# Weight conversion with its scratch in PSUM, and pair sums over fixed buffers, in an attention and gated-convolution kernel

## The chip, the cores and the metric

The kernel runs on one core of a Trainium2 chip. Its time is device microseconds (us) of one launch. A core has five engines with a queue each: TensorE (PE; PEld is its loading of stationary operands), VectorE (DVE), ScalarE (ACT), GpSimd (POOL) and SyncE (SP), which issues DMA transfers. Each works through its queue in order and waits on semaphores for the others. SBUF is the working memory, PSUM the memory that TensorE writes its results to. GpSimd has no operand in PSUM anywhere in this kernel.

## What is computed

Attention over 4 batches, 8 heads, 768 positions and 64 values a head, in which a query sees only the keys with the same 6 sign bits of a projection; then a gated feed-forward with a causal convolution of five taps.

```python
q_bits = (np.einsum('bhsd,dk->bhsk', q, proj) > 0)      # k_bits alike
mask = q_bucket[:, :, :, None] == k_bucket[:, :, None, :]
scores = np.where(mask, scale * np.matmul(q, k.transpose(0, 1, 3, 2)), -1000000000.0)
attn = np.exp(scores - np.max(scores, axis=-1, keepdims=True))
attn = attn / (np.sum(attn, axis=-1, keepdims=True) + 1e-09)
x = np.matmul(attn, v)                                   # heads side by side: (4, 768, 512)
gate_pre = sum(conv_w[k] * xp[:, k:k + S, :] for k in range(5))
out = (1.0 / (1.0 + np.exp(-gate_pre)) * (x @ w_val)) @ w_out
```

`w_val`, `w_out` (512 x 512 each) and `conv_w` arrive as float64, so the kernel receives them as 64-bit words and has to make fp32 out of them.

## The kernel before

The work is cut into 192 tiles: 32 units (batch, head) times 6 blocks of 128 queries. One step k of the main loop issues, for tile k: the row maximum over 768 scores on VectorE (`maxima`, L253), a factor and a shift a row (`factors` L259, `shifts` L263), the scores of tile k+1 on TensorE (`scores`, L247, two buffers `s` in PSUM), the exponentials on ScalarE with their row sum (`exponentials`, L271); every second step, for the pair of tiles k-2 and k-1, the row sums plus 1e-9 (`row_sums`, L277) and their reciprocal (`recip`, L281); for tile k-2 the division on GpSimd (`normalise`, L286); for tile k-3 the transposes on TensorE (L295, two halves of three, in two PSUM buffers `tp`), copied out by ScalarE in the step after (`keep_transposed`, L304). The product with the values (`attn_v`, L318), the split of its result into a high and a low part (`pair_x`, L338 and L339), the convolution (L347 and L349), and the feed-forward of a finished batch (`moe`, L380 and L405) are generators, and each step of the loop runs a step or a few of each.

The order in every queue is thus the order in which the Python code runs. It is written out by hand for TensorE, ScalarE, VectorE and GpSimd; the order of SyncE's transfers is found by the scheduler.

The conversion of the weights consists of eight parts of 128 x 512 (four of `w_val`, four of `w_out`). For each part a transfer of 512 KB brings the 64-bit words to a tile `w` (two buffers); ScalarE takes the magnitude of the upper word read as a float (L90, to a tile `o` in SBUF); VectorE bounds it from below (L92), shifts its bits (L93), joins them with the sign and exponent (L96), masks (L99) and scales the lower word (L100), then copies the high part out (L108); GpSimd forms the low part in two steps (L110, L112). The small `conv_w` takes the first five of these with 20 elements a row and an addition (L126). Two streams of four parts each take turns, and the loop runs (1, 0, 2, 0, 2, 2)[k % 6] steps from k = 0 on.

The sign bits of four heads at a time (`bits`, L203 and L206, twice half a row) go through one PSUM tile: `m` while no batch is in the feed-forward, else one of the two `tp` buffers. The tile `m` (one buffer) is otherwise the accumulator of the feed-forward, which begins after the first batch.

Of the kernel before, what the change touches and what calls it, by code (L numbers as in the profile page):

```python
# [8 lines left out]
FP32 = mybir.dt.float32  # L9
FP32R = mybir.dt.float32r  # L10
AF = mybir.ActivationFunctionType
ALU = mybir.AluOpType
AX = mybir.AxisListType
PSUM = bass.MemoryType.PSUM

I32 = mybir.dt.int32
# [10 lines left out]
def kernel(  # L27
# [49 lines left out]
    first = const.tile([P, 1], FP32, name="first")  # L77
    nc.scalar.activation(out=first, in_=ident[:, 0:1], func=AF.Exp)
    cw_sb = const.tile([P, NP * KW], FP32, name="cw_sb")

    wv = [const.tile([P, NP, 512], FP32R, name=f"wv{i}") for i in range(2)]
    wo = [const.tile([P, NP, 512], FP32R, name=f"wo{i}") for i in range(2)]

    def from_float64(w, t):

        lo, hi = w[:, :, 0], w[:, :, 1]
        a, d, ti = hi.bitcast(FP32), lo.bitcast(FP32), t.bitcast(I32)
        nc.scalar.activation(out=t, in_=a, func=AF.Abs)  # L90
        yield
        nc.vector.tensor_scalar(out=t, in0=t, scalar1=LEAST, scalar2=None, op0=ALU.max)  # L92
        nc.vector.tensor_scalar(out=ti, in0=ti, scalar1=3, scalar2=0x3fffffff,  # L93
                                op0=ALU.logical_shift_left, op1=ALU.bitwise_and)
        yield
        nc.vector.scalar_tensor_tensor(out=hi, in0=hi, scalar=-2 ** 30, in1=ti,  # L96
                                       op0=ALU.bitwise_and, op1=ALU.bitwise_or)
        yield
        nc.vector.tensor_scalar(out=ti, in0=hi, scalar1=-2 ** 23, scalar2=None, op0=ALU.bitwise_and)  # L99
        nc.vector.scalar_tensor_tensor(out=d, in0=lo.bitcast(U32), scalar=2.0 ** -52, in1=t,  # L100
                                       op0=ALU.mult, op1=ALU.mult)
        return a, d

    def split_weight(w, hi, lo):
        if w.dtype == I32:
            a, d = yield from from_float64(w, op.tile([P, 512], FP32, name="o"))
            yield
            nc.vector.tensor_copy(out=hi, in_=a)  # L108
            yield
            nc.gpsimd.tensor_tensor(out=a, in0=a, in1=hi.bitcast(FP32), op=ALU.subtract)  # L110
            yield
            nc.gpsimd.tensor_tensor(out=lo, in0=a, in1=d, op=ALU.add)  # L112
        else:
            nc.scalar.copy(out=hi, in_=w)
            yield
            nc.gpsimd.tensor_tensor(out=lo, in0=w, in1=hi.bitcast(FP32), op=ALU.subtract)

    def load_conv():
        if conv_w.dtype == mybir.dt.int64:
            w = const.tile([P, NP * KW, 2], I32, name="cw64")  # L120
            nc.sync.dma_start(out=w, in_=conv_w.bitcast(I32).rearrange("p (n t) -> p n t", t=2))
            t = const.tile([P, NP * KW], FP32, name="cwt")
            yield
            a, d = yield from from_float64(w, t)
            yield
            nc.vector.tensor_tensor(out=cw_sb, in0=d, in1=a, op=ALU.add)  # L126
        else:
            nc.sync.dma_start(out=cw_sb, in_=conv_w)

    def load_weights(which):  # L130
        parts = [(src[:, c, :], hl[0][:, c, :], hl[1][:, c, :])
                 for src, hl in ((w_val, wv), (w_out, wo)) for c in range(NP)]
        for src, hi, lo in parts[which::2]:
            if src.dtype == mybir.dt.int64:
                w = wst.tile([P, 512, 2], I32, name="w64")
                nc.sync.dma_start(out=w, in_=src.bitcast(I32).rearrange("p (n t) -> p n t", t=2))
            else:
                w = wst.tile([P, 512], FP32, name="w32")
                nc.sync.dma_start(out=w, in_=src)
            yield  # L140
            yield from split_weight(w, hi, lo)

    def load_raw(i):
        if i < len(units):
# [43 lines left out]
            yield from bits(i + 1)  # L188

    def side_tile():  # L190
        if not moes:
            return ps_m.tile([P, 512], FP32, name="m")
        return ps_t.tile([P, 512], FP32, name="tp")

    def bits(i):
# [69 lines left out]
    def exponentials(k):  # L265
        s, nb = ss.pop(k), nbs.pop(k)
        p = pp.tile([P, 2, HS], FP32, name="p")
        if k % 2 == 0:
            cur["sm"] = small.tile([P, 2, 2], FP32, name="sm")
        sm = cur["sm"]  # L270
        nc.scalar.activation(out=p, in_=s[:, :, 0:HS], func=AF.Exp, bias=nb, scale=gs.pop(k), accum_out=sm[:, k % 2, 0:1])  # L271
        ps[k] = (p.rearrange("p a b -> p (a b)"), sm)


    def row_sums(k):
        sums[k] = small.tile([P, 2, 2], FP32, name="s1")
        nc.vector.tensor_scalar(out=sums[k][:, :, 0], in0=ps[k][1][:, :, 0], scalar1=1e-9, scalar2=None, op0=ALU.add)  # L277

    def recip(k):
        ri = small.tile([P, 2], FP32, name="ri")  # L280
        nc.vector.reciprocal(out=ri, in_=sums.pop(k)[:, :, 0])  # L281
        rcs[k], rcs[k + 1] = ri[:, 0:1], ri[:, 1:2]

    def normalise(k):
# [80 lines left out]
    def moe(b, xs_, g):  # L365
        hs = {}
        todo = []

        def later():
            while todo:  # L370
                todo.pop(0)()

        def val(o, j):
            acc = acc_tile()
            m = 0
            for wi, xi in ((0, 0), (1, 0), (0, 1)):
                if m:
                    yield
                for c in range(NP):
                    nc.tensor.matmul(out=acc[:, 0:HS], lhsT=wv[wi][:, c, j * P:(j + 1) * P],  # L380
                                     rhs=xs_[(c, o)][xi], start=(m == 0), stop=(m == 11))
                    m += 1
                later()
            ht = hp.tile([P, HS], FP32, name="ht", bufs=2)
            nc.vector.tensor_tensor(out=ht, in0=acc[:, 0:HS], in1=g[j][:, o:o + HS], op=ALU.mult)  # L385

            def split():
                hh = hp.tile([P, HS], FP32R, name="hh")
                nc.vector.tensor_copy(out=hh, in_=ht)  # L389
                hl = hp.tile([P, HS], FP32R, name="hl")  # L390
                nc.gpsimd.tensor_tensor(out=hl, in0=ht, in1=hh.bitcast(FP32), op=ALU.subtract)  # L391
                hs[(o, j)] = (hh, hl)
            todo.append(split)
            yield

        def outp(o, tb):
            for gens in weights:
                finish(gens)
            acc = acc_tile()
            m = 0  # L400
            for hi, wi in ((0, 0), (0, 1), (1, 0)):
                if m:
                    yield
                for j in range(NP):
                    nc.tensor.matmul(out=acc, lhsT=hs[(o, j)][hi][:, tb * P:(tb + 1) * P],  # L405
                                     rhs=wo[wi][:, j, :], start=(m == 0), stop=(m == 11))
                    m += 1
                later()
            ob = op.tile([P, 512], FP32, name="o")
            if cur["gates"]:  # L410
                nc.vector.tensor_copy(out=ob, in_=acc)
            else:
                nc.scalar.copy(out=ob, in_=acc)
            r0 = o + tb * P
            nc.sync.dma_start(out=out[b, r0:r0 + P, :], in_=ob)
            yield

        def idle(n):
            for _ in range(n):
                later()  # L420
                yield

        def hold():
            while len(moes) < 2 and not cur["end"]:
                yield

        chunks = [(val, 0, j) for j in range(NP)]
        chunks += [(val, HS, 0)] + [(outp, 0, tb) for tb in range(3)] + [(val, HS, j) for j in range(1, NP)]
        chunks += [(idle, 2)] + [(outp, HS, tb) for tb in range(3)]
        if b < B - 1:  # L430
            chunks.insert(-2, (hold,))
        for f, *args in chunks:
            yield from f(*args)
# [9 lines left out]
    def step(gens):  # L443

        while gens:
            try:
                return next(gens[0])
            except StopIteration:
                gens.pop(0)

    def finish(gens):
        while gens:
            step(gens)
# [3 lines left out]
    with tc.manual_schedule(engines=ENGINES):  # L457
# [1 line left out]
            load_raw(i)  # L459
        load_values(0)  # L460
        first_prep()
        weights = [[load_conv(), load_weights(0)], [load_weights(1)]]
        first_signs()
        preps = [prep(1)]
        step(preps)
        scores(0)
        load_raw(5)
        step(weights[0])
        step(weights[1])
        turn = 0  # L470
        for k in range(N + LAG + 1):
            if 0 <= k - LAG - 1:
                keep_transposed(k - LAG - 1)
# [19 lines left out]
                exponentials(k)  # L493
            if k >= 60 or k % 2:
                step(convs)
            for _ in range((1, 0, 2, 0, 2, 2)[k % 6]):
                step(weights[turn])
                turn = 1 - turn
            for _ in range(3 if cur["gates"] else 1):
                step(moes)  # L500
            cur["gates"] = max(0, cur["gates"] - 1)
# [73 lines left out]
```

## Time and profile before

| | us |
|---|---|
| median of 3 runs | 630.7 |
| lowest and highest of them | 625.79, 632.56 |
| the profiled execution | 629.21 |
| its span, first to last instruction | 627.4 |
| busy: TensorE, VectorE, ScalarE, GpSimd | 591.0, 448.6, 421.2, 388.2 |

All shares and durations below are of that one profiled execution. A row of a group gives the line, the engine, the operation, what it writes and reads, how often, its busy time, the mean of one in ns, and the idle time of the engine just before it with what ended it. A row of a wait gives who waited for whom, the total, how often, and the longest. In order of time a row is a start, a duration, and what ran. Profiled spans on GpSimd are rough, and the ends of matmuls are modelled.

### The profile page before, as it was taken

Reading aid. Unit: us, or ns where it says so; the run is one execution under the profiler, and the core shown is the slowest. Engines: PE = TensorE matmul, PEld = TensorE weight load, DVE = VectorE, ACT = ScalarE, POOL = GpSimd, SP = SyncE. Lnnn points to the kernel's source line nnn. Section 1 sums busy time; section 2 is a strip of 40 time slices with the busy share of each in tenths; the row PEclk is TensorE's granted clock in tenths of the full one; section 3 lists DMA queues with packets and bytes.
Section 4 is the critical chain, followed back from the end, with each engine's and each line's share of the span. In section 5 each row is a group of like instructions: output and inputs, shape, how many; then the busy total and the mean of one; then the engine's idle time right before and its main releaser. Section 6 shows DMA issues by size and latency. Waiting matters only on the chain.

```text
span 627.4 us, 10639 instructions
## 1 busy us (share of the span) xinstructions
PE 591.0 (94%) x3496; PEld 425.8 (68%) x3496; DVE 448.6 (72%) x1032; ACT 421.2 (67%) x881; POOL 388.2 (62%) x358
## 2 busy tenths in 40 slices
PE   5799889989999999999999999999999999999997
PEld 2766556556667877677667777676667777776895
DVE  5879897989876857577676867569674877665532
ACT  3777767677788767577787667667788667675400
POOL 4677878687966856476655767367663677544221
PEclk9799988989999999999999999999999999999999
DMA  8542625343433343233434233243422224200111
GB/s 269 129 133 60 175 64 140 91 137 82 116 75 100 81 102 82 75 89 101 114 83 119 53 82 103 72 120 82 122 56 69 56 51 92 75 18 2 50 51 50
DMA packets 23270, 56.77 MB, mean 90 GB/s; under 512 B 4296, under 2 KB 4296, under 8 KB 23216
## 3 DMA queue, kind: packets, MB, share of 16 engines
q1 hardware_dynamic: 23072, 56.06, 33.7%
q8 instruction: 28, 0.46, 0.3%
q14 instruction: 26, 0.21, 0.1%
q10 hardware_dynamic: 144, 0.03, 0.0%
HBM read 23.12 MB, written 6.29 MB: 47 GB/s over the span
## 4 chain that ended last, share of the span: by engine, by line
PE 68%; DVE 13%; ACT 12%; DMA 3%; issue 2%; POOL 1%; SPq 0%; ACTq 0%; POOLq 0%; DVEq 0%
PE av L318 18%; PE s L247 16%; PE tp L295 12%; PE m L405 8%; PE m L380 7%; ACT p L271 5%; DVE nm L253 4%; ACT pt L304 4%; ACT x L326 2%; PE tp L380 1%; PE tp L405 1%; PE s L405 1%; DVE g L349 1%; DVE o L93 1%; PE tp L203 1%
## 5 line engine op out<-in xcount | busy, mean ns | idle before, releaser
L286 POOL TENSOR_SCALAR p<-p,ri 128x768 f32<-128x768 f32 x192 | 216.6, 1132 | 165.8 <-DVE nb L263 141.6
L253 DVE TENSOR_REDUCE nm<-s 128x1 f32<-128x768 f32 x192 | 182.5, 951 | 63.5 <-PE s L247 63.3
L304 ACT COPY pt<-tp 128x384 f32<-128x384 f32 x384 | 166.3, 485 | 84.2 <-PE tp L295 83.3
L271 ACT ACTIVATE p<-s,nb,gs 128x768 f32<-128x768 f32 x192 | 192.7, 1003 | 43.2 <-DVE nb L263 40.2
L295 PEld LDWEIGHTS tp<-ident,p 128*128 128x128 f32 x1152 | 131.6, 143 | 73.0 <-issue 45.7
L295 PE MATMUL tp<-ident,p 128*128 128x128 f32 x1152 | 166.8, 281 | 3.4 <-DVE u L206 1.5
L318 PE MATMUL av<-pt,vt 128*64 128x384 f32 x768 | 147.6, 506 | 0.0
L247 PE MATMUL s<-ak,aq 76*128 76x384 f32 x384 | 118.1, 389 | 23.9 <-ACT p L271 23.2
L247 PE MATMUL s<-bk,bq 128*128 128x384 f32 x384 | 100.6, 343 | 0.0
L318 PEld LDWEIGHTS av<-pt,vt 128*64 128x64 f32 x768 | 47.6, 137 | 63.8 <-issue 62.9
L247 PEld LDWEIGHTS s<-ak,aq 76*128 76x128 f32 x384 | 59.2, 194 | 38.0 <-ACT p L271 36.8
L349 DVE SCALAR_TENSOR_TENSOR g<-x,cw_sb,g 128x768 f32<-128x768 f32 x64 | 78.0, 1218 | 0.2
L247 PEld LDWEIGHTS s<-bk,bq 128*128 128x128 f32 x384 | 71.6, 193 | 0.0
L391 POOL TENSOR_TENSOR hl<-ht,hh 128x384 fp32r<-128x384 f32 x32 | 32.2, 1007 | 45.8 <-DVE hh L389 45.8
L169 POOL TENSOR_TENSOR bq<-r,aq 128x768 fp32r<-128x768 f32 x31 | 58.0, 1871 | 0.1
L326 ACT COPY x<-av 64x384 f32<-64x384 f32 x64 | 30.4, 475 | 34.0 <-PE av L318 33.3
L380 PE MATMUL m<-xh,wv 128*128 128x384 f32 x200 | 42.7, 337 | 0.0
L263 DVE TENSOR_SCALAR nb<-nm,gs 128x1 f32<-128x1 f32 x192 | 39.9, 208 | 3.5
L339 POOL TENSOR_TENSOR xl<-x,xh 128x384 fp32r<-128x384 f32 x32 | 33.6, 1067 | 12.2 <-DVE xh L338 12.2
L385 DVE TENSOR_TENSOR ht<-m,g 128x384 f32<-128x384 f32 x25 | 13.9, 556 | 35.3 <-PE m L380 32.0
L271 ACT ACTIVATION_READ_ACCUMULATOR p<-s,nb,gs 128x1 f32 x192 | 39.1, 204 | 0.0
L405 PE MATMUL m<-wo,hh 128*128 128x512 f32 x144 | 38.1, 394 | 0.0
(90 smaller groups left out, 489.8 us busy)
## 6 DMA issues: line engine op xcount, KB each, us to landing
r<-in_qk_dram SPq DMA_DIRECT2D x32, 384.0 KB
vt<-in_v_dram SPq DMA_DIRECT2D x16, 384.0 KB
out_dram<-o SPq DMA_DIRECT2D x24, 256.0 KB
ak<-aq SPq DMA_DIRECT2D x31, 192.0 KB
bk<-aq SPq DMA_DIRECT2D x31, 192.0 KB
bk<-bq SPq DMA_DIRECT2D x31, 192.0 KB
bq<-aq SPq DMA_DIRECT2D x31, 192.0 KB
w<-in_w_val_dram SPq DMA_DIRECT2D x4, 512.0 KB
```

The costliest lines, as they stand in the source:

```text
L169: nc.gpsimd.tensor_tensor(out=bq, in0=r, in1=aq.bitcast(FP32), op=ALU.subtract)
L247: nc.tensor.matmul(out=s[:, hf, 0:HS], lhsT=lq[0:n, qs], rhs=rk[0:n, hf * HS:(hf + 1) * HS], start=n == M, stop=n == P)
L253: nc.vector.tensor_reduce(out=nm, in_=s[:, :, 0:HS], axis=AX.XY, op=ALU.max, negate=True)
L271: nc.scalar.activation(out=p, in_=s[:, :, 0:HS], func=AF.Exp, bias=nb, scale=gs.pop(k), accum_out=sm[:, k % 2, 0:1])
L286: nc.gpsimd.tensor_scalar(out=p, in0=p, scalar1=rcs.pop(k), scalar2=1.0, op0=ALU.mult, op1=ALU.mult)
L295: nc.tensor.transpose(out=tp[:, n * P:(n + 1) * P], in_=p[:, kb * P:(kb + 1) * P], identity=ident)
L304: nc.scalar.copy(out=pt[:, :, qo:qo + P], in_=tp[:, 0:HS].rearrange("p (a b) -> p a b", b=P))
L318: nc.tensor.matmul(out=av[s * D:(s + 1) * D, 0:HS], lhsT=vt[:, kb, hh * D:(hh + 1) * D], rhs=pt[kb // 3][:, kb % 3, :], start=(kb == 0), s ...
L326: nc.scalar.copy(out=x[hh * D:(hh + 1) * D, o:o + HS], in_=av[s * D:(s + 1) * D, 0:HS])
L349: nc.vector.scalar_tensor_tensor(out=g, in0=x[:, k:k + S], scalar=w, in1=g, op0=ALU.mult, op1=ALU.add)
L380: nc.tensor.matmul(out=acc[:, 0:HS], lhsT=wv[wi][:, c, j * P:(j + 1) * P], rhs=xs_[(c, o)][xi], start=(m == 0), stop=(m == 11))
L405: nc.tensor.matmul(out=acc, lhsT=hs[(o, j)][hi][:, tb * P:(tb + 1) * P], rhs=wo[wi][:, j, :], start=(m == 0), stop=(m == 11))
```

## The change

Three things change.

The conversion's scratch moves. The magnitude stays in the SBUF tile `o`, and what VectorE makes from it (L97, L98, L104, and read by L101 and L105) lies in the PSUM tile `m`. The magnitude of the next part is taken one part ahead (`ahead`), right after GpSimd's first step of the part before, and its transfer is asked for after L101 of the part before. There is one stream instead of two, and no step of it runs before k = 8. The steps a turn are the same from there on.

The sums of the signs always go through a `tp` buffer, since `m` is now the scratch.

The row sums of a pair of tiles go to one of four fixed tiles `sm` of 2 x 2 elements a row, filled with 1e-9 once. The exponentials write column 0, the constant stays in column 1, and the addition of 1e-9 becomes a sum along the last axis (L298).

```diff
+    sms = [const.tile([P, 2, 2], FP32, name=f"sm{i}") for i in range(4)]
+    for sm in sms:
+        nc.gpsimd.memset(sm, 1e-9)
...
+    def magnitudes(w, t):
+        nc.scalar.activation(out=t, in_=w[:, :, 1].bitcast(FP32), func=AF.Abs)
+        return t
...
-        nc.scalar.activation(out=t, in_=a, func=AF.Abs)
-        yield
-        nc.vector.tensor_scalar(out=t, in0=t, scalar1=LEAST, scalar2=None, op0=ALU.max)
+        nc.vector.tensor_scalar(out=t, in0=m, scalar1=LEAST, scalar2=None, op0=ALU.max)
...
-            a, d = yield from from_float64(w, op.tile([P, 512], FP32, name="o"))
+            a, d = yield from from_float64(w, m, ps_m.tile([P, 512], FP32, name="m"))
...
             nc.gpsimd.tensor_tensor(out=a, in0=a, in1=hi.bitcast(FP32), op=ALU.subtract)
+            ahead()
             yield
...
+        def ahead():
+            if loads:
+                w = loads.pop(0)
+                m = magnitudes(w, op.tile([P, 512], FP32, name="o")) if w.dtype == I32 else None
+                ready.append((w, m))
+
+        loads = [fetch(parts[0][0])]
+        yield
+        ahead()
+        for n, (_, hi, lo) in enumerate(parts):
+            yield
+            for i, _ in enumerate(split_weight(*ready.pop(0), hi, lo, ahead)):
+                if i == 1 and n + 1 < len(parts):
+                    loads.append(fetch(parts[n + 1][0]))
+                yield
...
     def side_tile():
-        if not moes:
-            return ps_m.tile([P, 512], FP32, name="m")
         return ps_t.tile([P, 512], FP32, name="tp")
...
-        if k % 2 == 0:
-            cur["sm"] = small.tile([P, 2, 2], FP32, name="sm")
-        sm = cur["sm"]
+        sm = sms[k // 2 % 4]
...
-        sums[k] = small.tile([P, 2, 2], FP32, name="s1")
-        nc.vector.tensor_scalar(out=sums[k][:, :, 0], in0=ps[k][1][:, :, 0], scalar1=1e-9, scalar2=None, op0=ALU.add)
+        sums[k] = small.tile([P, 2], FP32, name="s1")
+        nc.vector.tensor_reduce(out=sums[k], in_=ps[k][1], axis=AX.X, op=ALU.add)
...
-        weights = [[load_conv(), load_weights(0)], [load_weights(1)]]
+        weights = [load_conv(), load_weights()]
...
-            for _ in range((1, 0, 2, 0, 2, 2)[k % 6]):
-                step(weights[turn])
-                turn = 1 - turn
+            for _ in range((1, 0, 2, 0, 2, 2)[k % 6] if k >= 8 else 0):
+                step(weights)
```

VectorE's queue among the first tiles, from the maximum of tile 6 to that of tile 7, before (`nm` is the negated maximum, `gs` and `nb` factor and shift, `ri` the reciprocal; numbers behind a name tell buffers apart):

```order
L253 TENSOR_REDUCE nm<-s 128x1
L277 TENSOR_SCALAR s_339<-sm 128x2
L259 TENSOR_SCALAR gs<-nm 128x1
L281 RECIPROCAL ri<-s_339 128x2
L263 TENSOR_SCALAR nb<-nm,gs 128x1
L99 TENSOR_SCALAR o<-w_186 128x512
L100 SCALAR_TENSOR_TENSOR w_186<-w_186,o 128x512
```

and the same tile after:

```order
L276 TENSOR_REDUCE nm<-s 128x1
L298 TENSOR_REDUCE s_333<-sm_120 128x2
L282 TENSOR_SCALAR gs<-nm 128x1
L302 RECIPROCAL ri<-s_333 128x2
L286 TENSOR_SCALAR nb<-nm,gs 128x1
```

The two conversion steps between the shift of tile 6 and the maximum of tile 7 are gone from there; the addition of L277 is the sum of L298.

VectorE's queue at tile 38, behind the shift, where a part of `w_out` and the first half of the signs meet, before:

```order
L281 RECIPROCAL ri<-s_1474 128x2
L263 TENSOR_SCALAR nb<-nm,gs 128x1
L99 TENSOR_SCALAR o<-w_1273 128x512
L100 SCALAR_TENSOR_TENSOR w_1273<-w_1273,o 128x512
L206 TENSOR_SCALAR u<-m,packed 128x384
```

and after:

```order
L302 RECIPROCAL ri<-s_1467 128x2
L286 TENSOR_SCALAR nb<-nm,gs 128x1
L101 SCALAR_TENSOR_TENSOR w_1268<-w_1268,m 128x512
L104 TENSOR_SCALAR m<-w_1268 128x512
L105 SCALAR_TENSOR_TENSOR w_1268<-w_1268,m 128x512
L229 TENSOR_SCALAR u<-tp,packed 128x384
```

Three steps of one part stand ahead of the reading of the signs (`u`) instead of two, and the signs are read from `tp`.

TensorE's queue at the same place, before (`r` holds a head's queries and keys):

```order
L203 MATMUL m<-r,proj_sb 32x384 x4
L295 MATMUL tp<-ident,p 128x128 x6
L247 MATMUL s<-ak,aq 128x384 x2
L247 MATMUL s<-bk,bq 128x384 x2
L203 MATMUL m<-r,proj_sb 32x384 x4
```

and after:

```order
L226 MATMUL tp<-r,proj_sb 32x384 x4
L316 MATMUL tp<-ident,p 128x128 x6
L270 MATMUL s<-ak,aq 128x384 x2
L270 MATMUL s<-bk,bq 128x384 x2
L226 MATMUL tp<-r,proj_sb 32x384 x4
```

The order is the same, but the sums of the signs now take a buffer between two pairs of transposes, whose second half comes to the same buffer next.

More of the change, by code (lines that the diff above doesn't have):

```diff
@@ L79, with from_float64 @@
     cw_sb = const.tile([P, NP * KW], FP32, name="cw_sb")
+    sms = [const.tile([P, 2, 2], FP32, name=f"sm{i}") for i in range(4)]
+    for sm in sms:
+        nc.gpsimd.memset(sm, 1e-9)
     wv = [const.tile([P, NP, 512], FP32R, name=f"wv{i}") for i in range(2)]
     wo = [const.tile([P, NP, 512], FP32R, name=f"wo{i}") for i in range(2)]
-    def from_float64(w, t):
+    def magnitudes(w, t):
+        nc.scalar.activation(out=t, in_=w[:, :, 1].bitcast(FP32), func=AF.Abs)
+        return t
+    def from_float64(w, m, t):
         lo, hi = w[:, :, 0], w[:, :, 1]
         a, d, ti = hi.bitcast(FP32), lo.bitcast(FP32), t.bitcast(I32)
-        nc.scalar.activation(out=t, in_=a, func=AF.Abs)
-        yield
-        nc.vector.tensor_scalar(out=t, in0=t, scalar1=LEAST, scalar2=None, op0=ALU.max)
+        nc.vector.tensor_scalar(out=t, in0=m, scalar1=LEAST, scalar2=None, op0=ALU.max)
         nc.vector.tensor_scalar(out=ti, in0=ti, scalar1=3, scalar2=0x3fffffff,
@@ L102, in from_float64, with split_weight @@
         return a, d
-    def split_weight(w, hi, lo):
+    def split_weight(w, m, hi, lo, ahead):
         if w.dtype == I32:
-            a, d = yield from from_float64(w, op.tile([P, 512], FP32, name="o"))
+            a, d = yield from from_float64(w, m, ps_m.tile([P, 512], FP32, name="m"))
             yield
@@ L113, in split_weight @@
         else:
-            nc.scalar.copy(out=hi, in_=w)
+            nc.vector.tensor_copy(out=hi, in_=w)
+            ahead()
             yield
@@ L123, in load_conv @@
             yield
-            a, d = yield from from_float64(w, t)
+            a, d = yield from from_float64(w, magnitudes(w, const.tile([P, NP * KW], FP32, name="cwm")), t)
             yield
@@ L128, in load_conv, with load_weights, fetch @@
             nc.sync.dma_start(out=cw_sb, in_=conv_w)
-    def load_weights(which):
+    def load_weights():
         parts = [(src[:, c, :], hl[0][:, c, :], hl[1][:, c, :])
                  for src, hl in ((w_val, wv), (w_out, wo)) for c in range(NP)]
-        for src, hi, lo in parts[which::2]:
+        def fetch(src):
             if src.dtype == mybir.dt.int64:
@@ L139, in load_weights @@
                 nc.sync.dma_start(out=w, in_=src)
+            return w
+        ready = []
+        def ahead():
[5 more added lines that the diff above has]
+        yield
+        ahead()
+        for n, (_, hi, lo) in enumerate(parts):
             yield
-            yield from split_weight(w, hi, lo)
+            for i, _ in enumerate(split_weight(*ready.pop(0), hi, lo, ahead)):
+                if i == 1 and n + 1 < len(parts):
+                    loads.append(fetch(parts[n + 1][0]))
+                yield
     def load_raw(i):
@@ L275, in row_sums @@
     def row_sums(k):
-        sums[k] = small.tile([P, 2, 2], FP32, name="s1")
-        nc.vector.tensor_scalar(out=sums[k][:, :, 0], in0=ps[k][1][:, :, 0], scalar1=1e-9, scalar2=None, op0=ALU.add)
+        sums[k] = small.tile([P, 2], FP32, name="s1")
+        nc.vector.tensor_reduce(out=sums[k], in_=ps[k][1], axis=AX.X, op=ALU.add)
     def recip(k):
         ri = small.tile([P, 2], FP32, name="ri")
-        nc.vector.reciprocal(out=ri, in_=sums.pop(k)[:, :, 0])
+        nc.vector.reciprocal(out=ri, in_=sums.pop(k))
         rcs[k], rcs[k + 1] = ri[:, 0:1], ri[:, 1:2]
@@ L396, in outp @@
         def outp(o, tb):
-            for gens in weights:
-                finish(gens)
+            finish(weights)
             acc = acc_tile()
@@ L467 @@
         load_raw(5)
-        step(weights[0])
-        step(weights[1])
-        turn = 0
+        for gen in weights:
+            next(gen)
         for k in range(N + LAG + 1):
```

## The prediction

> **What bounds the kernel now.** I read the page first (busy shares and the row of granted clock), then the trace by stages, then what ended the engines' waits in the one slow stage, then its groups of instructions and its order of time. From the page, the span, the busy shares and the granted TensorE clock in 40 slices:
>
> ```profile
> span 627.4 us, 10639 instructions
> PE 591.0 (94%) x3496; PEld 425.8 (68%) x3496; DVE 448.6 (72%) x1032; ACT 421.2 (67%) x881; POOL 388.2 (62%) x358
> PEclk9799988989999999999999999999999999999999
> ```
>
> TensorE is busy 94% of the span, and its clock is below full only in the first quarter. The change works in that quarter, so it has to be looked at alone. A step k of the main loop is one tile of 128 queries with one row maximum (L253), so counting L253 in a stretch of time counts tiles (columns: stretch, its length, busy time and count, clock, DMA):
>
> ```profile
> 10.40:28.00 17.60, 7.60 (x8) 0.81 0.63 162
> 28.00:141.00 113.00, 37.95 (x40) 0.94 0.43 115
> 141.00:170.00 29.00, 11.38 (x12) 1.00 0.40 102
> ```
>
> The same stretches with all engines, and the rest of the loop:
>
> ```profile
> core 0: us, PE busy (x) PEld busy (x) DVE busy (x) ACT busy (x) POOL busy (x), PEclk, DMA share, GB/s
> 10.40:28.00 17.60, 13.08 (x63) 10.83 (x61) 16.38 (x42) 11.27 (x24) 9.23 (x8) 0.81 0.63 162
> 28.00:141.00 113.00, 100.48 (x587) 65.54 (x586) 98.75 (x221) 84.31 (x181) 86.08 (x77) 0.94 0.43 115
> 141.00:170.00 29.00, 26.59 (x163) 17.98 (x161) 26.28 (x60) 23.09 (x52) 25.07 (x23) 1.00 0.40 102
> 170.00:585.50 415.50, 407.52 (x2476) 296.19 (x2476) 287.77 (x678) 294.62 (x616) 254.17 (x236) 1.00 0.31 79
> ```
>
> From 170 us on TensorE is busy 407.52 of 415.50 us and VectorE 287.77: nothing that this change does to VectorE can show there beyond the 8 us that TensorE is idle. From 28 to 141 us a tile takes 113/40 = 2.825 us; from 141 to 170 us, where the weights are nearly done and the other work of a tile is of the same kind, 29/12 = 2.417 us. The difference, 0.408 x 40 = 16.3 us, is what the conversion of the weights costs in that stretch. The waits there say how:
>
> ```profile
> ACT p L271 <- DVE nb L263: 14.8, 16, 2.1
> PE s L247 <- ACT p L271: 12.2, 17, 2.4
> ```
>
> TensorE waits for the exponentials to free a score buffer, and these wait for VectorE's shift (nb), which is late because conversion steps stand ahead of the next maximum in VectorE's queue. In order of time, one such place (start, duration):
>
> ```profile
> 85.86 1.54 DVE L349 SCALAR_TENSOR_TENSOR g<-x,cw_sb,g 128x768 f32<-128x768 f32 x1
> 87.32 1.31 DVE L96 SCALAR_TENSOR_TENSOR w<-w,o 128x512 int32<-128x512 int32 x1
> 88.55 0.94 DVE L253 TENSOR_REDUCE nm<-s 128x1 f32<-128x768 f32 x1
> 91.17 1.01 PE L247 MATMUL s<-ak,aq 76*128 76x384 f32 x2 [2.33 <-ACT p L271]
> ```
>
> The convolution step and L96 hold VectorE for 2.85 us, the maximum comes after them, and TensorE stands 2.33 us.
>
> **The change part by part.** *Scratch in PSUM.* The five instructions whose operands move, in the stretch 28 to 141 us (count, busy, mean ns), and ahead of them the commonest 512-element VectorE row that reads PSUM:
>
> ```profile
> L411 DVE COPY o<-m 128x512 f32<-128x512 f32 x6 | 4.2, 692 | 17.1 <-PE m L405 17.1
> ...
> L93 DVE TENSOR_SCALAR o<-o 128x512 int32<-128x512 int32 x7 | 7.2, 1026 | 0.2
> L100 DVE SCALAR_TENSOR_TENSOR w<-w,o 128x512 f32<-128x512 uint32 x6 | 7.1, 1184 | 0.2
> L96 DVE SCALAR_TENSOR_TENSOR w<-w,o 128x512 int32<-128x512 int32 x6 | 6.2, 1040 | 0.0
> L92 DVE TENSOR_SCALAR o<-o 128x512 f32<-128x512 f32 x7 | 4.5, 648 | 1.2 <-ACT o L90 1.2
> L99 DVE TENSOR_SCALAR o<-w 128x512 int32<-128x512 int32 x6 | 2.5, 417 | 0.0
> ```
>
> One part of the weights costs 1026 + 1184 + 1040 + 648 + 417 = 4315 ns of VectorE. L99 and L93 have the same shape and form, and one takes 417, the other 1026; the 20-element L93 says that this is not the length:
>
> ```profile
> L93 DVE TENSOR_SCALAR cwt<-cwt x1: 839/839/839, 15.7 to 15.7; 128x20 int32<-128x20 int32 x1
> ```
>
> Where I looked, L93 starts while GpSimd is in an instruction that began a moment earlier, and L99 does not; so I take the excess as waiting for GpSimd, which goes when the scratch is in PSUM. In exchange a one-operand instruction at 417 becomes one like L411. With 692 for all five, a part costs 3460, so 0.855 us less, 6.8 us over 8 parts. No row shows VectorE writing PSUM, or reading and writing one PSUM tile (the new L98): the bounds are 417 from below (L99) and, from above, today's 1026 for each of the two. [...]
>
> What of this reaches the end: the five rows sum to 27.5 us in the stretch and the stretch lost 16.3 us, so 0.59 us shows per us of them. *The start moved to k = 8.* The one part that was converted in the first 8 tiles now comes later, so from k = 8 on there are 8 x 3.46 = 27.7 us instead of 7 x 4.315 = 30.2: 2.5 x 0.59 = 1.5 us gained. I do not take more, since three dependent steps (L97, L98, L101, some 2.1 us) now stand in one turn of one tile, and such a lump costs what exceeds TensorE's 2.4 us a tile; with lumps alone it could be 3 us lost, and with all of the 6.8 showing it is 6.8 gained. In the first tiles I read the gain in order of time:
>
> ```profile
> 24.56 0.52 PE L247 MATMUL s<-bk,bq 128*128 128x384 f32 x2
> 25.10 0.42 DVE L99 TENSOR_SCALAR o<-w 128x512 int32<-128x512 int32 x1
> 25.55 1.28 DVE L100 SCALAR_TENSOR_TENSOR w<-w,o 128x512 f32<-128x512 uint32 x1
> 26.75 0.95 DVE L253 TENSOR_REDUCE nm<-s 128x1 f32<-128x768 f32 x1
> 29.36 1.01 PE L247 MATMUL s<-ak,aq 76*128 76x384 f32 x2 [1.32 <-ACT p L271]
> ```
>
> The scores of tile 7 are there at 25.08 and their maximum starts at 26.75, 1.67 us late, and two tiles on TensorE stands 1.32 us. The other conversion steps among the first tiles stand while TensorE is behind. I take 2.0 us, bounds 1.3 and 2.7.
>
> *Sign sums in the transposes' buffers.* The half sums of the signs that used tile m (six of them, at k = 14, 15, 38, 39, 62, 63) now take one of the two tp buffers, so the second half of the next transposes waits until VectorE has read the sums (u). Before, eight halves late in the loop already ran so:
>
> ```profile
> L206 DVE TENSOR_SCALAR u<-tp,packed 128x384 fp32r<-128x384 f32 x8 | 5.4, 677 | 8.7 <-PE tp L203 8.4
> ...
> PE tp L295 <- DVE u L206: 1.5, 4, 0.4
> ```
>
> That is 0.2 us of TensorE a half, where VectorE had time to spare. In the first quarter VectorE runs late: at k = 38, L101, L104 and L105 stand ahead of u, 3 x 0.69 + 0.68 = 2.75 us. Behind the waiting transposes stand the next scores, but VectorE has the next maximum to do meanwhile, so I stay near the row: 0.3 us a half, 1.8 in all; bounds 1.1 and 16.5 (six times 2.75).
>
> *Magnitudes ahead.* ScalarE still takes 8 of them, from a transfer asked for three turns earlier at the least, and its queue holds exponentials and copies behind one that waits. One part is asked for at k = 28 and read at k = 29. Before, the only such wait was:
>
> ```profile
> ACT o L90 <- DMA w<-in_w_val_dram: 0.8, 1, 0.8
> ```
>
> I take 0.5 us, bounds 0 and one tile, 2.4. SyncE issues the same 8 transfers; each still waits for GpSimd to finish with its buffer, and is now asked for later than that, so it holds up its queue less: nothing taken. GpSimd's two steps a part stay, and its four fills of the new constants (four elements each) stand where it waits for the first input: nothing.
>
> *Pair sums.* 96 additions become 96 sums of two along the last axis:
>
> ```profile
> L277 DVE TENSOR_SCALAR s<-sm 128x2 f32<-128x2 f32 x96 | 19.0, 198 | 5.5 <-ACT p L271 4.9
> L281 DVE RECIPROCAL ri<-s 128x2 f32<-128x2 f32 x96 | 15.9, 166 | 0.8
> ```
>
> I price the new one like the reciprocal, 166: 32 ns less, and only the 30 before 170 us count: 30 x 0.032 x 0.59 = 0.6, taken as 0.5. If it costs 0.25 us, it loses about 0.9; if a few long ones go in the TensorE-bound part, it gains 1.5. One buffer fewer to recycle frees nothing that any engine waited for.
>
> The sum: -2.0 - 1.5 + 1.8 + 0.5 - 0.5 = -1.7 us. The profiled execution took 629.21 us (its span 627.4), so 627.5. The median of the runs shown is 630.7, 1.5 above it and inside their spread of 625.79 to 632.56. That spread is 1.1% of the time, so about 1%, 6.3 us, is what a measurement of this kernel can tell from no change.
>
> **The rivals.** *VectorE stops setting the pace* (faster). If all 6.8 us show and the start gives 2.7, less the 1.8 and with the other half us terms cancelling: 629.2 - 7.7 = 621.5. For it speaks that VectorE is busy 98.75 of 113 us there; against it, that the steps still come in lumps. *The clock comes back* (faster). The granted clock is 0.81 and 0.94 in the first two stretches, so TensorE loses 17.6 x 0.19 + 113 x 0.06 = 10.1 us of full speed; half of that on the path and gone, beside the sum, gives 622.5. [...] *The sums' wait* (slower). If each of the six halves costs the 2.75 us of VectorE's backlog, 16.5 instead of 1.8 stands in the sum: 642.2. It turns the result to over 1% slower from about 1.9 us a half on. Against it speaks the 0.2 of the eight halves before. *The PSUM scratch does not do what it says* (same). If L93's excess is a fixed cost of its two integer operations, L98 takes 692 + 609 = 1.30 us; 8 x 0.61 x 0.59 = 2.9 us more: 630.4.
>
> **How the numbers follow.** The sum's own case 0.62 (within 1%), VectorE's pace 0.13, the clock 0.09, the sums' wait 0.09, the fixed cost 0.07. Faster by over 1% (under 624.4 against the median) hold the second and third, 0.22; slower (over 637.0) the fourth and a little of the last, 0.10; within 1% remains 0.68. The range goes from 620.0, just below both faster cases, to 636.0, which leaves out the sums' wait and the tails.
>
> **What would show it.** Right: L97, L98, L101, L104 and L105 near 692 with little scatter; 8 tiles in under 16 us after 10.4 us; between k = 8 and 53 still about 2.75 us a tile, with TensorE still waiting on the exponentials; waits of the transposes on u ten times instead of four, none over 1 us; the pair sums near 166 without the long ones. Wrong: L98 at 1.3 us (the fixed cost); a full clock from 28 to 141 us; a wait of ScalarE's magnitudes on their transfer of 2 us or more; anything that moves the 415 us after 170 us, where I count on nothing.

## The result

The changed kernel takes 625.0 us (median of 15 runs, 623.79 to 626.13), the kernel before 628.05 us in the runs made beside it (15 runs, 625.75 to 632.56). The ratio is 0.9943, with a 95% interval of 0.9926 to 0.9960: 0.6% faster. That is clear of no change, where the prediction took about 1% to be the least that a measurement could tell. The profiled execution of the changed kernel took 624.6 us.

From its page, the span, the busy shares and the granted clock in 40 slices:

```profile
span 622.8 us, 10649 instructions
PE 587.7 (94%) x3496; PEld 422.6 (68%) x3496; DVE 437.3 (70%) x1032; ACT 420.6 (68%) x881; POOL 376.3 (60%) x362
PEclk9799999999999999999999999999999999999999
```

VectorE and GpSimd have each lost 11 to 12 us of work, and the clock is low in the second slice only, where before it was low in four. The same stretches of time as before, counted by the row maximum (now L276), and with all engines:

```profile
10.40:28.00 17.60, 8.60 (x9) 0.81 0.62 168
28.00:141.00 113.00, 39.83 (x42) 1.00 0.44 118
141.00:170.00 29.00, 11.34 (x12) 1.00 0.41 101
```

Nine tiles instead of eight by 28 us, then 42 instead of 40 up to 141 us (2.69 us a tile), with the clock at 1.00 there instead of 0.94. What the engines waited for from 28 to 141 us:

```profile
ACT p L292 <- DVE nb L286: 11.1, 16, 1.6
PE s L270 <- ACT p L292: 9.7, 18, 1.1
```

TensorE still waits for the exponentials, and these for VectorE, but 9.7 us instead of 12.2, and the longest time is 1.1 us, where it was 2.4. The conversion rows and the pair sums of that stretch:

```profile
L98 DVE TENSOR_SCALAR m<-m 128x512 int32<-128x512 int32 x8 | 5.6, 699 | 0.3
L105 DVE SCALAR_TENSOR_TENSOR w<-w,m 128x512 f32<-128x512 uint32 x8 | 5.5, 691 | 0.3
L104 DVE TENSOR_SCALAR m<-w 128x512 int32<-128x512 int32 x8 | 5.5, 689 | 0.1
L97 DVE TENSOR_SCALAR m<-o 128x512 f32<-128x512 f32 x8 | 5.5, 687 | 0.6 <-ACT o L90 0.5
L101 DVE SCALAR_TENSOR_TENSOR w<-w,m 128x512 int32<-128x512 int32 x8 | 5.5, 684 | 0.3
...
L298 DVE TENSOR_REDUCE s<-sm 128x2 f32<-128x4 f32 x21 | 3.1, 147 | 1.4 <-ACT p L292 1.3
```

All five stand within some 2% of each other: 3450 ns a part where it was 4315. GpSimd gained too. In the same stretch, its normalisation and its first copy of a head before, and then after (same columns):

```profile
L286 POOL TENSOR_SCALAR p<-p,ri 128x768 f32<-128x768 f32 x41 | 45.9, 1123 | 23.4 <-DVE nb L263 21.4 <-DVE o L99 1.0 <-ACT x L326 0.6
...
L166 POOL CAST aq<-r 128x768 fp32r<-128x768 f32 x6 | 7.3, 1208 | 0.0
```

```profile
L307 POOL TENSOR_SCALAR p<-p,ri 128x768 f32<-128x768 f32 x43 | 42.3, 990 | 23.2 <-DVE nb L286 16.4 <-DVE cwt L104 3.5 <-PE tp L316 3.2
...
L191 POOL CAST aq<-r 128x768 fp32r<-128x768 f32 x7 | 5.8, 823 | 0.0
```

Nothing was changed in these two. With the scratch back in SBUF and all else as changed (below), they take 1092 and 1005 ns, so most of the first gain and about half of the second go with the place of the scratch.

Where the time went, from the starts of the row maxima in the profiled executions (us from the maximum of one tile to that of another, and from tile 60 to the end of the span). The last column counts the stretches of 3.41 us at half clock up to 610 us; the first experiment explains them:

| kernel | tiles 0 to 12 | 12 to 48 | 48 to 60 | 60 to the end | low stretches |
|---|---|---|---|---|---|
| before | 28.6 | 102.0 | 29.0 | 457.3 | 6 |
| after | 27.2 | 97.3 | 28.8 | 458.9 | 2 |
| after, scratch in SBUF | 26.7 | 108.8 | 29.1 | 458.8 | 5 |
| after, steps from k = 0 | 32.8 | 96.9 | 30.0 | 458.9 | 6 |
| after, old sums | 28.3 | 100.7 | 29.3 | 458.4 | 3 |
| before, one stream | 33.5 | 103.4 | 30.0 | 458.2 | 4 |
| before, start at k = 8 | 25.9 | 103.7 | 33.8 | 457.4 | 5 |
| after, spread | 24.3 | 95.7 | 30.2 | 459.4 | 2 |
| after, bits left out | 25.1 | 92.7 | 30.0 | 459.0 | 2 |

The first quarter gives 6.3 us, and some 1.5 us are lost again behind it. These two executions lie 4.6 us apart, the medians 3.05.

### The profile page after: what moved, and what is told of

It is laid out like the page before. It is cut to its first block, busy times and chain, and to the rows that moved or that the text cites. A ratio compares the mean times of both kernels' runs of the same rounds, so it can differ in the third digit from the quotient of the medians.

```text
span 622.8 us, 10649 instructions
## 1 busy us (share of the span) xinstructions
PE 587.7 (94%) x3496; PEld 422.6 (68%) x3496; DVE 437.3 (70%) x1032; ACT 420.6 (68%) x881; POOL 376.3 (60%) x362
## 4 chain that ended last, share of the span: by engine, by line
PE 69%; ACT 16%; DVE 9%; issue 2%; DMA 1%; POOL 1%; SPq 0%; ACTq 0%; DVEq 0%; POOLq 0%
PE av L339 19%; PE s L270 16%; PE tp L316 13%; PE m L425 8%; ACT p L292 7%; PE m L401 7%; ACT pt L325 5%; DVE nm L276 3%; ACT x L347 3%; PE tp L226 2%; PE tp L425 1%; PE s L425 1%; PE s L401 1%; PE tp L401 1%; DVE g L370 1%
## 5 line engine op out<-in xcount | busy, mean ns | idle before, releaser
L307 POOL TENSOR_SCALAR p<-p,ri 128x768 f32<-128x768 f32 x192 | 208.4, 1090 | 166.1 <-DVE nb L286 142.4
L276 DVE TENSOR_REDUCE nm<-s 128x1 f32<-128x768 f32 x192 | 182.5, 951 | 63.3 <-PE s L270 63.0
L316 PEld LDWEIGHTS tp<-ident,p 128*128 128x128 f32 x1152 | 129.8, 141 | 75.9 <-issue 48.1
L339 PE MATMUL av<-pt,vt 128*64 128x384 f32 x768 | 144.9, 499 | 0.0
L270 PE MATMUL s<-ak,aq 76*128 76x384 f32 x384 | 116.6, 385 | 20.0 <-ACT p L292 19.2
L412 POOL TENSOR_TENSOR hl<-ht,hh 128x384 fp32r<-128x384 f32 x32 | 32.2, 1005 | 47.9 <-DVE hh L410 47.9
```

Source lines behind the costliest of these rows:

```text
L270: nc.tensor.matmul(out=s[:, hf, 0:HS], lhsT=lq[0:n, qs], rhs=rk[0:n, hf * HS:(hf + 1) * HS], start=n == M, stop=n == P)
L276: nc.vector.tensor_reduce(out=nm, in_=s[:, :, 0:HS], axis=AX.XY, op=ALU.max, negate=True)
L307: nc.gpsimd.tensor_scalar(out=p, in0=p, scalar1=rcs.pop(k), scalar2=1.0, op0=ALU.mult, op1=ALU.mult)
L316: nc.tensor.transpose(out=tp[:, n * P:(n + 1) * P], in_=p[:, kb * P:(kb + 1) * P], identity=ident)
L339: nc.tensor.matmul(out=av[s * D:(s + 1) * D, 0:HS], lhsT=vt[:, kb, hh * D:(hh + 1) * D], rhs=pt[kb // 3][:, kb % 3, :], start=(kb == 0), s ...
```

## The experiments

Theory 1 is that of the prediction: VectorE's load sets the pace of the first quarter, and the shorter rows and the free first tiles carry the gain. The rivals: the gain is the clock's; and the single parts do something else than was priced. Times are medians, and each ratio is against runs of the kernel before made beside them on the same chip. Where two kernels that did not run beside each other are compared, the difference of their ratios times 629 us is taken.

**The kernel before, again.** No edit.

> The kernel before, unchanged, to see its own spread. Theory 1 (VectorE's load sets the pace of the first quarter): 628 us, the clock of a run says little about its time. Rival (the clock): the mean granted clock differs from run to run (0.983 in the profile of before, 0.995 in that of after), and the time follows it, about 1.5 us for each 0.003.

Measured: 629.13 us, ratio 1.0007 (0.9987 to 1.0027). Together with the 29 runs of the kernel before made beside them, by the mean granted clock of the run (four runs at other values left out):

```
clock        0.980   0.983   0.986   0.989   0.992
runs             8      10      10       5       4
median us    630.4   629.3   628.1   628.5   626.1
```

The same program runs between 625.7 and 632.9 us, and its time goes with its clock, as the rival said (with 1.5 us for each 0.003) and Theory 1 did not. In the traces' clock records the clock is full or half (1.00 or 0.50), and inside the loop it is half for 3.41 us or a whole multiple (3.41 or 6.83 us in the profiles of before and after). One such window is 1.7 us of 629, or 0.003 of the mean clock, and with it the time is longer by about 1 us (correlation -0.87 over the 41 runs). The changed kernel ran 11 times at 0.995 (median 624.9) and 3 times at 0.992 (median 625.9). So at 0.992 the two kernels cannot be told apart: 626.1 and 625.9 (626.3 over all 12 runs of the kernel before at 0.992 in this document). On these few runs the changed kernel's gain in the median is that it no longer falls into low windows behind the start. Two such places in the profile of before, each as the 3.41 us ahead of the fall and the low stretch itself (the clock is the third number from the end):

```profile
87.29:90.70 3.41, 1.54 (x12) 1.27 (x10) 3.38 (x9) 1.42 (x3) 1.55 (x2) 1.00 0.42 92
90.70:97.52 6.82, 6.36 (x21) 3.93 (x22) 4.94 (x11) 4.10 (x11) 6.26 (x6) 0.50 0.35 74
124.83:128.24 3.41, 1.04 (x8) 0.66 (x6) 3.38 (x8) 1.83 (x4) 2.12 (x2) 1.00 0.54 115
128.24:131.65 3.41, 3.41 (x12) 1.42 (x12) 3.34 (x10) 1.60 (x4) 2.85 (x3) 0.50 0.30 66
```

TensorE is busy 1.54 and 1.04 of the 3.41 us (first pair after the length), and then the clock is 0.50. So it is in every trace here: all 30 falls of the clock between 14 and 600 us come right behind 3.41 us in which TensorE was busy at most 57.1%, and only 6 of the 2315 other such stretches at full clock were as idle. In the changed kernel none from 28 to 170 us is under 70%. That the low windows follow TensorE's idle times is thus shown. What a window costs is read from the spread of the runs; no run held the clock fixed.

**Scratch back in SBUF**, everything else as changed:

```diff
-            a, d = yield from from_float64(w, m, ps_m.tile([P, 512], FP32, name="m"))
+            a, d = yield from from_float64(w, m, scr.tile([P, 512], FP32, name="sc"))
```

> The changed kernel with the conversion's scratch in a tile of SBUF instead of PSUM; everything else as changed. Theory 1: the five conversion rows go back from 3.45 to about 4.3 us a part, L98 to 1.0 us, and 6.8 us of VectorE x 0.59 = 4 us come back: 629 us. Rival (what helped is the later start and the clock): 625 to 626 us, though the rows are long again.

Measured: 636.45 us, ratio 1.0122 (1.0099 to 1.0145): 11 us slower than the changed kernel and 7 slower than before, far more than the 4 expected. Its rows from 28 to 141 us:

```profile
L106 DVE SCALAR_TENSOR_TENSOR w<-w,sc 128x512 f32<-128x512 uint32 x7 | 7.8, 1107 | 0.2
...
L99 DVE TENSOR_SCALAR sc<-sc 128x512 int32<-128x512 int32 x7 | 6.5, 927 | 0.2
L102 DVE SCALAR_TENSOR_TENSOR w<-w,sc 128x512 int32<-128x512 int32 x7 | 6.3, 895 | 0.2
L98 DVE TENSOR_SCALAR sc<-o 128x512 f32<-128x512 f32 x7 | 6.2, 889 | 0.1
...
L105 DVE TENSOR_SCALAR sc<-w 128x512 int32<-128x512 int32 x7 | 5.1, 731 | 0.1
```

4549 ns a part, 1.1 us more than in PSUM, 8.8 us over eight parts, and even the mask that took 417 ns before (here L105) now takes 731. GpSimd's normalisation there is slow as well:

```profile
L308 POOL TENSOR_SCALAR p<-p,ri 128x768 f32<-128x768 f32 x39 | 42.4, 1092 | 25.7 <-DVE nb L287 22.1 <-DVE cwt L105 3.5
```

So the scratch in PSUM is worth 11 us in this order of steps, more than one us for each us of VectorE's rows. All of it stands between tiles 12 and 48 (108.8 against 97.3 us). It is not VectorE's rows alone, though. The median clock of these runs is 0.9855 against 0.995, which by the 41 runs goes with some 3 us, and GpSimd's busy time rose from 376.3 to 384.9 us. The runs do not part the three.

**Old pair sums**, in the changed kernel:

```diff
-        sm = sms[k // 2 % 4]
+        if k % 2 == 0:
+            cur["sm"] = small.tile([P, 2, 2], FP32, name="sm")
+        sm = cur["sm"]
...
-        nc.vector.tensor_reduce(out=sums[k], in_=ps[k][1], axis=AX.X, op=ALU.add)
+        nc.vector.tensor_scalar(out=sums[k][:, :, 0], in0=ps[k][1][:, :, 0], scalar1=1e-9, scalar2=None, op0=ALU.add)
```

> The changed kernel with the pair sums as before (an addition of 1e-9 to two sums in a recycled tile). Theory 1: 50 ns each on VectorE, of which only the 30 in the first quarter count: 625.0 + 0.9 = 625.9 us. Rival (the few long ones of 0.4 to 0.9 us stand in the chain to the exponentials also later): 627 us or more.

Measured: 628.24 us, ratio 0.9983 (0.9966 to 1.0000): 2.5 us by the ratios. The rival is nearer. By the 41 runs some 1 us of it goes with the clock, which was 0.992 in 8 of these 12 runs and 0.995 in 11 of 15 of the changed kernel. The row from 28 to 141 us, and then all 96 (least, median, longest in ns; first and last start):

```profile
L297 DVE TENSOR_SCALAR s<-sm 128x2 f32<-128x2 f32 x20 | 7.5, 377 | 1.3 <-ACT p L291 1.3
```

```profile
L297 DVE TENSOR_SCALAR s<-sm x96: 150/159/1811, 16.5 to 570.3; 128x2 f32<-128x2 f32 x96
```

Half of them take 159 ns or less, and one 1811, with two elements a row. In order of time, that one:

```profile
93.77 1.81 POOL L191 TENSOR_TENSOR bq<-r,aq 128x768 fp32r<-128x768 f32 x1
93.80 1.81 DVE L297 TENSOR_SCALAR s<-sm 128x2 f32<-128x2 f32 x1
95.53 0.14 DVE L279 TENSOR_SCALAR gs<-nm 128x1 f32<-128x1 f32 x1
```

It starts just behind an instruction of GpSimd and ends with it. The 59 additions that start with GpSimd idle take 151 to 170 ns, and every longer one starts inside an instruction of GpSimd. The addition stands between the maximum and the shift, so everything behind it waits. The sum along the last axis, in the same place, takes 139 to 158 ns in all 96 cases, 37 of which start inside an instruction of GpSimd.

**Steps from k = 0**, in the changed kernel:

```diff
-            for _ in range((1, 0, 2, 0, 2, 2)[k % 6] if k >= 8 else 0):
+            for _ in range((1, 0, 2, 0, 2, 2)[k % 6]):
```

> The changed kernel with the conversion's steps from k = 0 on instead of k = 8. If the later start is worth what the first tiles show (tile 12 comes 1.2 us earlier than before), 626.2 us; if it only moves the load, 625.0 us; the steps then end 8 tiles earlier.

Measured: 630.42 us, ratio 1.0029 (1.0014 to 1.0043): 5.4 us slower, more than either number. All of it is in the first 12 tiles (32.8 against 27.2 us). In order of time there:

```profile
13.62 0.18 DVE L97 TENSOR_SCALAR cwt<-cwm 128x20 f32<-128x20 f32 x1 [1.32 <-ACT cwm L90]
...
17.32 0.82 DVE L104 TENSOR_SCALAR cwt<-cw 128x20 int32<-128x20 int32 x1
18.17 0.84 DVE L105 SCALAR_TENSOR_TENSOR cw<-cw,cwt 128x20 f32<-128x20 uint32 x1
...
19.53 0.94 DVE L276 TENSOR_REDUCE nm<-s 128x1 f32<-128x768 f32 x1
...
24.43 0.69 DVE L97 TENSOR_SCALAR m<-o 128x512 f32<-128x512 f32 x1 [1.69 <-ACT o L90]
```

In one stream the first magnitudes are asked for in the same turn as the step that reads them. VectorE stands 1.32 and 1.69 us for ScalarE, which has exponentials ahead of them, and the next maxima stand behind. Two of the 20-element steps, whose scratch stays in SBUF, take 0.8 us. TensorE's clock pays as well:

```profile
10.40:28.00 17.60, 12.52 (x45) 10.24 (x43) 13.21 (x34) 8.46 (x17) 5.89 (x6) 0.61 0.58 163
```

0.61 in place of 0.81. So the later start mends what the one stream breaks at the start.

**Parts of the change alone, in the kernel before.** The sums of the signs through tp:

```diff
     def side_tile():
-        if not moes:
-            return ps_m.tile([P, 512], FP32, name="m")
         return ps_t.tile([P, 512], FP32, name="tp")
```

> The kernel before with one part of the change alone: the sums of the signs always through a tp buffer. As predicted, 0.3 us for each of six halves: +1.8, 631.0 us. Rival (the transposes wait for VectorE's whole backlog): +5 us or more, 634 us.

Measured: 629.27 us, ratio 1.0016 (0.9995 to 1.0037), so +1.0 us with an interval from -0.3 to 2.3. The pair sums over the fixed tiles (the reverse of the edit above):

> The kernel before with one part of the change alone: the pair sums along the last axis over the fixed tiles. As predicted, -0.5 to -1 us, 628.5 us, since in the first quarter the old form took 191 ns on the mean there. Rival (worth as much as in the changed kernel, where the old form took 377 ns there): -3 us, 626 us.

Measured: 628.38 us, ratio 1.0010 (0.9989 to 1.0032): no gain to be seen. No step before k = 8:

```diff
-            for _ in range((1, 0, 2, 0, 2, 2)[k % 6]):
+            for _ in range((1, 0, 2, 0, 2, 2)[k % 6] if k >= 8 else 0):
```

> The kernel before with one part of the change alone: no conversion step before k = 8. If the later start is worth the 5.4 us that its undoing cost in the changed kernel, 624 us; if that holds only where the steps are short, the load is moved into tiles that are full already: 628 to 630 us.

Measured: 632.62 us, ratio 1.0074 (1.0044 to 1.0103): 4.7 us slower. The first 12 tiles gain 2.7 us, and tiles 12 to 60 lose 6.5. The two streams now reach to tile 60, and their five rows got longer as well, 4931 ns a part on the mean of all eight instead of 4272. One stream, with magnitude and transfer ahead (the new `split_weight` and `load_weights` with the scratch in SBUF, and all else as before):

```diff
-        weights = [[load_conv(), load_weights(0)], [load_weights(1)]]
+        weights = [load_conv(), load_weights()]
```

> The kernel before with one part of the change alone: one stream with the magnitude and the transfer taken ahead (scratch in SBUF, steps from k = 0, old sums, signs through m while the first batch has no feed-forward). If the parts add up, it must cost what the others overpay: after - before is -4 us, the scratch gave -11, the start -5, the sums -3, the signs +2, so +13 us, 642 us. As predicted for lumps (three dependent steps in one turn), +3 us: 632 us.

Measured: 638.54 us, ratio 1.0158 (1.0132 to 1.0184): 10 us slower, near the 13 that adding up asked for and far from the 3 of the prediction. 4.9 us of it are in the first 12 tiles.

**Single steps, spread over the tiles.** In the changed kernel, one VectorE instruction to a step, put where a tile has no convolution step or signs:

```diff
+    def turns(k):
+        if k < 8:
+            return 0
+        if k in (14, 38, 39):
+            return 0
+        if k < 24:
+            return 1 + k % 2
+        if k % 2 == 0:
+            return 2 if k in (48, 54, 60) else 1
+        return {1: 1, 11: 2}.get(k % 12, 0)
...
         nc.vector.tensor_scalar(out=t, in0=m, scalar1=LEAST, scalar2=None, op0=ALU.max)
+        yield
...
         nc.vector.tensor_scalar(out=ti, in0=hi, scalar1=-2 ** 23, scalar2=None, op0=ALU.bitwise_and)
+        yield
...
-            for _ in range((1, 0, 2, 0, 2, 2)[k % 6] if k >= 8 else 0):
+            for _ in range(turns(k)):
                 step(weights)
```

Besides, the small weights' magnitude has a step of its own, the copy and GpSimd's first step share one, as do GpSimd's second and the next part's first, and the transfer is asked for one step earlier.

> The changed kernel with the conversion cut into single VectorE instructions, one to a turn, put into tiles that have no convolution step or signs to read (ending by k = 62), the transfers asked for one step earlier. If lumps are what the one stream costs: counting per tile what VectorE's queue holds over 2.41 us, tiles 8 to 61 hold 18.9 us in the changed kernel and 10.3 here, so -8.6 us: 616 us. Rival (VectorE's sum of work alone sets the pace; it is the same 130 us): 625 us.

Measured: 622.39 us, ratio 0.9885 (0.9860 to 0.9911): faster than both kernels, 3.6 us below the changed one by the ratios, and over 1% below the kernel before. Its tiles:

```profile
10.40:28.00 17.60, 8.61 (x9) 0.81 0.65 171
28.00:133.00 105.00, 38.08 (x40) 1.00 0.43 118
133.00:162.00 29.00, 11.43 (x12) 1.00 0.44 118
```

40 tiles in 105 us, 2.63 us each. The lumps are a price, but not 8.6 us of it. The clock of these runs, 0.992 to 0.994, is no higher than the changed kernel's, so this gain is not the clock's.

**The bit instructions left out.**

> The changed kernel without its five bit instructions on each 128 x 512 part (the high parts are then copies of the raw upper words, the low parts sums of these; magnitudes, copies, transfers and GpSimd's two steps stay): what is left of the conversion's price. By lumps, 18.9 - 4.5 = 14.4 us less: 611 us. By the changed kernel's own stages (tiles 8 to 48 at 2.705 us, tiles 48 to 60 at 2.40): 0.305 x 40 = 12 us less, 613 us. If something other than VectorE holds that quarter (the sums of the signs, GpSimd): 620 us or more.

Measured: 620.6 us, ratio 0.9854 (0.9829 to 0.9880), 5.6 us below the changed kernel where 12 to 14 were expected. From 28 us on:

```profile
28.00:133.00 105.00, 98.02 (x605) 63.62 (x603) 78.97 (x198) 84.94 (x187) 80.28 (x79) 1.00 0.46 124
```

VectorE is busy 75% of the time and TensorE 93%: without these 27.6 us of VectorE's work the quarter is mostly TensorE's. The spread kernel has 3.6 of the 5.6 us that taking them out gives.

**The spread kernel with scratch in SBUF** (the edit of the scratch, above):

> The spread kernel with the conversion's scratch in SBUF instead of PSUM. In the one-stream kernel that cost 11 us. If the price is VectorE's longer rows (some 1.1 us a part, 8.8 us in all) wherever they stand: 622.4 + 9 = 631 us. If single instructions fit into what their tiles leave free, or start where GpSimd is idle: 625 us or less, and PSUM is then not needed. Times of runs are also read against their granted clock: in 29 runs of the kernel before, 0.003 less of it goes with 1 us more.

Measured: 626.33 us, ratio 0.9971 (0.9956 to 0.9985): 5.4 us above the spread kernel, half of the 11. Two of its rows from 26 to 145 us:

```profile
L98 DVE TENSOR_SCALAR sc<-o 128x512 f32<-128x512 f32 x7 | 6.0, 859 | 2.8 <-ACT o L91 2.8
...
L100 DVE TENSOR_SCALAR sc<-sc 128x512 int32<-128x512 int32 x6 | 3.5, 592 | 0.0
```

The shift (L100), 1026 ns in the kernel before, takes 592 when it stands in another tile than the bound (L98), and the bound, 648 before, takes 859. The single instances say why. Of the eight shifts the four that start with GpSimd idle take 416 to 429 ns, and the four that start inside an instruction of GpSimd take 720 to 1014. So how long such a row is depends on where it stands beside GpSimd's work. Over all eight parts the five rows take 3950 ns a part here, 0.5 us more than in PSUM: 4.0 us in all, where 8.8 were expected.

**The spread kernel with old sums** (the edit of the sums, above):

> The spread kernel with the pair sums as before. In the one-stream kernel that cost 3.2 us, with 8 additions of 0.46 to 1.8 us in the first quarter; in the kernel before nothing. If the cost comes with the scratch in PSUM, which leaves GpSimd running when the addition comes: 3 us again, 625.5 us. If it comes from the tiles with three conversion steps: 1 us or less, 623 us.

Measured: 622.81 us, ratio 0.9914 (0.9894 to 0.9933), 1.8 us above the spread kernel by the ratios, between the two answers; the intervals (each about 1.5 us wide to a side) do not settle it.

## Why the prediction was right or wrong

It said 627.5 us, within 1%, and the time is 625.0, inside the range, with the small gain on the right side. That is in good part luck. The sum came out because two large effects of opposite sign, which it had far too small, cancel. What was left of the gain went with the granted clock, which the sum did not hold. And two of its own signs of being wrong came: a full clock from 28 to 141 us, and a change behind 170 us.

- *VectorE's rows.* Right: 684 to 699 ns instead of the 692 taken, 3450 ns a part instead of 3460. That L93's excess was waiting for GpSimd held: in the kernel before all eight start inside an instruction of GpSimd (930 to 1145 ns), and all eight of L99 with GpSimd idle (416 to 418 ns). The shift takes 698 to 700 ns in PSUM, where seven of the eight start inside an instruction of GpSimd, 592 on the mean in another place in SBUF, and its 20-element form 176 ns in the changed kernel where it took 839. The rival of a fixed cost falls.
- *What reaches the end.* This step failed. One us of VectorE was priced at 0.59 us of time wherever it stands. Leaving out 27.6 us gave 5.6 us, 0.2 for each, while 8.8 us of longer rows went with 11 us, and 4.0 us of them in the spread kernel with 5.4. This fits VectorE's work being nearly free up to the room that TensorE's 2.4 us a tile leaves, and dear beyond it, so that a mean price says nothing near that edge. It is not shown alone, since GpSimd's work is longer too with the scratch in SBUF (384.9 us against 376.3). Besides, the 16.3 us behind the 0.59 hold four low windows of the clock (from 29.3 us, two from 90.7, from 128.2), by the 41 runs some 4 us that were put down to VectorE's rows. The term of -1.5 us took the shorter rows and the lumps together. Measured apart they are -11 and +10 (the latter with the steps from k = 0), each outside its bounds of -6.8 to +3, and together about -1.
- *The order of steps.* The prediction named the three dependent steps in one turn and put them at up to 3 us, inside the term of the scratch. As a part of its own the one stream cost 10 us with its scratch in SBUF. Half of that is in the first 12 tiles, where VectorE waits in order for ScalarE's magnitudes (1.32 and 1.69 us in the run from k = 0); the prediction looked there for a wait on the transfer (0.5 us; none is in the trace) and not for a wait on ScalarE.
- *The later start.* -2.0 us was taken. The first 12 tiles gave 2.7 us in the kernel before and 5.6 us in the changed one. The load that comes back later cost 6.5 us with the two streams in SBUF. So its sign depends on the other parts.
- *The signs.* +1.8 us taken, +1.0 measured alone (-0.3 to 2.3). The waits in the changed kernel:

```profile
PE tp L316 <- DVE u L229: 2.3, 6, 0.4
```

  Six waits, where ten were foreseen, none above 0.4 us. The rival of the whole backlog falls.
- *The pair sums.* -0.5 us taken. Alone in the kernel before they gave nothing (0.6 us the other way, interval -0.7 to 2.0), and in the changed kernel 2.5. The price of 166 ns was near (147); what was missed is that the old form would have become worse, 377 ns on the mean, once the order of steps changed.
- *The clock.* The rival had 0.09 and 5 us. The low windows from 28 us on did go, and with 1 us for each the change from 0.983 or 0.986 to 0.995 is worth the 3 to 4 us that were gained. At the same clock, 0.992, the two kernels took the same time (626.1 and 625.9 us, on few runs). So the rival was right and should have had the larger chance, though the price of a window rests on the spread of the runs. It is not apart from the rest: the windows follow TensorE's idle times (busy at most 57.1% of the 3.41 us ahead of each of the 30 falls), and the longest wait for the exponentials from 28 to 141 us went from 2.4 to 1.1 us.
- *Behind 170 us* the prediction counted on nothing. From tile 60 to the end the changed kernel is some 1.5 us slower, and every kernel with one stream is slower there than those with two (458.2 to 459.4 us against 457.3 to 457.8). The signs and the sums alone account for some 0.4 us each. What the rest is stays open; it was not tried.

That the scratch in PSUM alone would help two streams was not tried: their steps alternate, so two scratch tiles would have to be alive, and there is one tile m.

## What to carry to other kernels

Where an engine is close to the pace, as VectorE is here (98.75 of 113 us before), the price of its work need not be a mean (5.6 us gained with 27.6 left out; 11 us lost with 8.8 added, GpSimd's and the clock's share among them): measure it from both sides, once with the work left out and once with it made longer, before adding up terms, and compare runs at the same granted clock. Parts of such a change do not add; the start at k = 8 lost 5 us alone and gained 5 with the other parts, so a part is judged in the kernel that it will live in. A small VectorE instruction in a chain (two elements a row) is best in a form that stays short while GpSimd works (here the sum along the last axis, 139 to 158 ns, where the addition took up to 1811), and long steps are best put one at a time into the tiles that have room (3.6 us by the ratios here).

## What the runs showed of the hardware

- A VectorE addition over two elements a row took 150 to 1811 ns in SBUF (old pair sums, 96 of them), and a sum along the last axis over the same data 139 to 158 ns (the changed kernel, 96 of them). Only additions that start inside an instruction of GpSimd are long: the 59 that start with GpSimd idle took 151 to 170 ns. Of the sums along the last axis 37 start inside one, and none of them is longer than 158 ns. Two elements are enough for an addition to be long.
- With the scratch alone moved from SBUF to PSUM, GpSimd's normalisation went from 1092 to 990 ns and its copy from 1005 to 823.
- VectorE reading and writing one PSUM tile in place (L98) took 698 to 700 ns for 512 elements, about as long as from PSUM to SBUF (692).
- The spread of the kernel before, 625.7 to 632.9 us, goes for the most part with its clock: about 1 us for each 3.41 us window at half speed (correlation -0.87 over 41 runs). Such a window came behind 3.41 us in which TensorE was busy 57% or less, and the longest wait of TensorE for the exponentials was 2.4 us (before, 28 to 141 us), so none of those waits filled a window alone.
